# A filter dealt anew over the partitions of a spectral-mixing and feed-forward kernel, with a pause in SyncE's queue and three plane copies on VectorE

## The chip, the cores and the metric

The kernel runs on one core of one Trainium2 chip. The core has five engines with queues of their own: TensorE (matmuls, in the profile PE, its weight loads PEld), VectorE (DVE), ScalarE (ACT), GpSimd (POOL) and SyncE (SP), which here only issues DMAs. GpSimd issues DMAs as well. Sixteen DMA engines carry all transfers. Instructions of one queue run in order, and queues wait for each other by semaphores. The metric is the device time of one execution in microseconds, and the median of the runs is what is compared.

## The reference

The input x is 2048 rows of 576 bfloat16 values. The first part is a spectral mixing layer: layer norm over each row, a two-dimensional real Fourier transform over rows and columns, an elementwise product with a complex filter of 2048 x 289, the inverse transform, and a residual addition. The second part is a feed-forward block with a gate: layer norm, two products with 576 x 4608 weights, GELU of the one times the other, a product with 4608 x 576, and again a residual addition.

```
X = rfft2(layernorm(x));  X = X * (w_r + 1j * w_i)
h = x + irfft2(X)
n = layernorm(h)
out = h + (gelu(n @ w_gate) * (n @ w_up)) @ w_down
```

`w_r` and `w_i` are the two planes of the filter. They are inputs in device memory and have to be loaded.

## The kernel before, in words

Both transforms are written as matmuls with constant tables. The transform of length 2048 over the rows is split as 128 x 16: `A` stages (line 551) make 64 frequencies with 128-row tables while x is loaded and normalised; `D` (line 640) transforms over the columns, `B` (line 660) does the length-16 part with table BT, `T` (line 673, VectorE) multiplies by the filter, `V` and `R` (lines 681 and 698) go back over the length-16 part with table VT, `I` (line 835) goes back over the columns, and `N` (line 852) over the rest of the rows. After that come the second layer norm, the gate and up products (line 944) and the down product (line 1044).

Work between `B` and `V` is done in 16 groups; group number g runs from 1 to 15 and then 0. The filter lies in the tile WS as [partition, jp, plane, g, column]. The 128 partitions are two halves of 64, and jp (0 or 1) says which half's rows a DMA brings. Of the 64 rows of a half, 32 are "up" rows, which lie in memory in rising order of g and are brought by `w_up` (line 449), and 32 are "down" rows, in falling order, brought by `w_down` (line 456), 16 rows in a DMA, one for each of four slots `sl`. Row g = 0 of the down rows has its own DMAs, `w_zero` (line 464). Before, the up rows lie on the first 32 partitions of a half and the down rows on the other 32. Where a row lies must agree with the tables BT and VT, whose rows are put in the same order in `build_tables` (line 143).

The filter comes in two halves of g (`hf`): g 0 to 8 first (call it the first filter half), g 9 to 15 second. `T` needs the whole filter on all 128 partitions for both jp, so every half of 64 partitions is copied to the other one by `dup_w` (line 719), in four pieces k of g: k = 0 is g 1 to 5, k = 1 is g 6 to 8, k = 2 is g 9 to 12, k = 3 is g 13 to 15 and 0. Piece 0 is copied by engines (line 728 VectorE, line 730 GpSimd), one instruction per jp and plane; pieces 1 to 3 are copied by DMAs that GpSimd issues (line 242 is the helper by which every DMA is issued).

The order of the work is written out by hand in strings of tokens (`SEQ1`, `SEQF`, `SEQ`). Each engine gets its instructions in program order, and `Prog.emit` puts a wait before an instruction for each last writer or reader of what it touches. All DMAs under one semaphore name count on one semaphore, so a reader waits for all of that name issued so far.

SyncE's queue around the change is: loads of x and the table ATB, the tables FT and BT, the first filter half (plane 1, then plane 0), part of VT, the second filter half, the zero rows; then three small transfers VR<-RB of the transform's remaining columns; then, in `tab_load` (line 754), a wait for the last `dup_w` DMA and the tables VT, DT, IT and IDT; then six more VR<-RB, and the feed-forward weights. GpSimd's queue is: copies and scaling for the first layer norm, two loads of the second filter half (plane 0, slots 2 and 3), the two copies of piece 0 for plane 1, the two DMAs of piece 1, seven small operations (line 745), the six DMAs of pieces 2 and 3, and then its share of VR<-RB. VectorE copies piece 0 of plane 0 (two instructions) after the last U casts (line 562) and before the casts and products of the `D` to `V` stages.

Of the kernel before, what the change touches and what calls it, by code (L numbers as in the profile page):

```python
# [9 lines left out]
S, D, K2 = 2048, 576, 289  # L10
# [36 lines left out]
def build_tables():  # L47
# [52 lines left out]
    for st in range(2):  # L100
        g = 1 - st
        for p in range(128):
            half, r, jj = p // 64, (p % 64) // 4, p % 4
            low = (g + 16 * jj) if half == 0 else _minus_rows(g)[jj]
            k = 128 * r + low
            w = np.exp(-2j * np.pi * ((k * nn) % 2048) / 2048.0)
            if low in (0, 64):
                sl, ri = 0, (0 if low == 0 else 1)
# [8 lines left out]
            if half == 0:  # L117
                sl = jj
                e = np.exp(-2j * np.pi * ((r * nn) % 16) / 16.0)
                ca, cb = e, 1j * e  # L120
            else:
                sl = (128 - low - g) // 16
# [17 lines left out]
    for st in range(2):  # L140
        for jp in range(2):
            for q in range(64):
                half, r, sl = q // 32, (q % 32) // 2, 2 * jp + q % 2
                jj = sl if half == 0 else (4 - sl) % 4 if st else 3 - sl
                po, cut = 64 * half + 4 * r + jj, slice(2 * jp, 2 * jp + 2)
                for m in range(2):
                    for ri in range(2):
                        BN[jp, :, :, st, m, ri, q] = B[st, m + ri, :, cut, :, po].reshape(16, 4)
                for ri in range(2):
                    VN[st, jp, ri, q, 0] = V[st, ri, po, :, :, cut].reshape(2, 16, 4)  # L150
                    VN[st, jp, ri, q, 1] = (1 - 2 * ri) * V[st, 1 - ri, po, :, :, cut].reshape(2, 16, 4)
# [180 lines left out]
def _build(nc, A_x, A_w_r, A_w_i, B_w_gate, B_w_up, B_w_down, out):  # L332
    P = Prog(nc)
    T = build_tables()
    dram = {n: nc.inline_tensor(_np_bf16(T[n]), name="c_" + n.lower()) for n in T}
    PE, DVE, ACT, SP, POOL = "pe", "dve", "act", "sp", "pool"
# [12 lines left out]
    WS = sb.alloc("WS", [128, 2, 2, NG, K2], BF16)  # L349
# [96 lines left out]
    P.dma(SP, FT[:, :, :].rearrange("p a b -> p (a b)"), dram["FTAB"][:, :], "ft", w=["FT"])  # L446
    P.dma(SP, BT[:, :, :, :].rearrange("p a b c -> p (a b c)"), dram["BTAB"][:, :], "bt", w=["BT", "BT1"])

    def w_up(pl, hf):
        g0, g1 = ((0, 9), (9, 16))[hf]  # L450
        src = (A_w_r, A_w_i)[pl].tensor
        for jp in range(2):
            P.dma(SP, WS[64 * jp:64 * jp + 32, jp, pl, g0:g1, :].rearrange("p g k -> p (g k)"),
                  bass.AP(src, (32 * jp + g0) * K2, [[128 * K2, 16], [16 * K2, 2], [1, (g1 - g0) * K2]]), f"w{pl}{hf}", w=[("W", hf, pl, jp)])

    def w_down(pl, hf, sls=(0, 1, 2, 3), eng=SP, sem=""):
        g0, g1 = ((1, 9), (9, 16))[hf]
        src = (A_w_r, A_w_i)[pl].tensor
        for sl in sls:
            p0 = 64 * (sl // 2) + 32  # L460
            P.dma(eng, WS[p0 + sl % 2:p0 + 32:2, sl // 2, pl, g0:g1, :], bass.AP(src, (64 + 16 * (3 - sl) + 16 - g0) * K2, [[128 * K2, 16], [-K2, g1 - g0], [1, K2]]),
                  f"w{pl}{hf}{sem}", w=[("W", hf, pl, 2 + sl)])

    def w_zero(pl):
        for jp in range(2):
            P.dma(SP, WS[64 * jp + 32:64 * jp + 64, jp, pl, 0, :], bass.AP((A_w_r, A_w_i)[pl].tensor, (64 + 32 * jp) * K2, [[128 * K2, 16], [(-16 if jp else 48) * K2, 2], [1, K2]]),
                  f"wz{pl}", w=[("W", 2, pl, jp)])

    for pl in (1, 0):
        w_up(pl, 0)  # L470
        w_down(pl, 0)
    P.dma(SP, VT[:, 0:2, :, :].rearrange("p a b c -> p (a b c)"), dram["VTAB"][:, 0:512], "vt", w=["VT", "VT1"])
    for pl in (1, 0):
        w_up(pl, 1)
        w_down(pl, 1, (0, 1, 2, 3) if pl else (0, 1))
    for pl in (1, 0):
        w_zero(pl)
    GORD = list(range(1, NG)) + [0]
    wkeys = [[("W", hf, pl, h) for pl in range(2) for h in range(6 if hf < 2 else 2)] for hf in range(3)]

# [109 lines left out]
    for t, w in enumerate(SEQF):  # L592
        k, i = w[0], w[1:].rstrip("abc")
# [125 lines left out]
    def dup_w(k, jp, pl=slice(0, 2), eng=None):  # L719
        a, b = 64 * jp, 64 - 64 * jp  # L720
        n = ("Wd", k, jp, pl.start)
        for g0, g1 in (((1, 6),), ((6, 9),), ((9, 13),), ((13, 16), (0, 1)))[k]:
            dst, src = (WS[q:q + 64, jp, pl, g0:g1, :].rearrange("p a g k -> p a (g k)")[:, :, 1:] for q in (b, a))
            r = [x for x in (wkeys[1] if g0 > 8 else wkeys[0] if g0 else wkeys[0] + wkeys[2]) if pl.start <= x[2] < pl.stop]
            if eng is None:
                op = P.dma(POOL, dst, src, f"wd{k}{jp}", r=r, w=[(*n, g0)])
            elif eng == DVE:
                P.op(DVE, lambda v: v.tensor_copy(dst, src), r=r, w=[(*n, g0)])
            else:
                P.op(POOL, lambda v: v.tensor_scalar(dst, src, 1.0, 1.0, op0=ALU.mult, op1=ALU.mult), r=r + [("ATS", NT - 1)], w=[(*n, g0)])  # L730
        return op if eng is None else None

    w_down(0, 1, (2, 3), POOL, "p")
    for jp in range(2):
        dup_w(0, jp, slice(1, 2), POOL)
        dup_w(0, jp, slice(0, 1), DVE)
    for jp in range(2):
        dup_w(1, jp)
    c = 0
    while c < NT:  # L740
        c1 = c + 1
        while c not in ACT_TILES and c1 < NT and c1 not in ACT_TILES:
            c1 += 1
        src, f, keys = (SA[:, 0, c:c1], -1.0 / D, "SA0") if c in ACT_TILES else (MV1[:, c:c1, 0], -1.0, "MV1")
        P.op(POOL, lambda g, c=c, c1=c1, src=src, f=f: g.tensor_scalar(NM[:, c:c1], src, f, 1.0, op0=ALU.mult, op1=ALU.mult),
             r=[(keys, k) for k in range(c, c1)], w=[("NM", k) for k in range(c, c1)])
# [63 lines left out]
    for t, w in enumerate(SEQ):  # L810
        k, i = w[0], int(w[1:].rstrip("ADSP"))
# [207 lines left out]
    for j, c in enumerate(range(NPRE, NT)):  # L1019
        f = DEF0 + DSTEP * j  # L1020
# [77 lines left out]
def bass_sequential_preLN__spectral_gfnet__geglu_ffn__prompt_kernel(  # L1098
    nc, A_x, A_w_r, A_w_i, B_x, B_w_gate, B_w_up, B_w_down, out
):  # L1100
    _build(nc, A_x, A_w_r, A_w_i, B_w_gate, B_w_up, B_w_down, out)
# [28 lines left out]
```

## Time and profile before

| | |
|---|---|
| median of 3 runs | 485.8 us (484.93 to 485.94) |
| profiled execution | 486.04 us, span 484.2 us |
| granted TensorE clock | 1.00 |
| PE busy | 477.1 us (99%) |
| VectorE, ScalarE, GpSimd busy | 182.8, 145.4, 53.2 us |
| DMA | 33.19 MB in 28438 packets |

The span runs from the first to the last instruction of the program; the profiled execution's own time has 1.8 us around it. Lines L123 are those of the kernel's source. In a timeline row stand the start, the duration, the engine, the line, the operation, what is written and read, the shapes and the count, and in square brackets how long the engine had been idle and what ended that. SPq is SyncE's queue. In the chain of waits stand the start, the duration and what the time went to. In the groups of DMA issues stand the count, the size of each, and the median time from issue to landing.

### The profile page before, as it was taken

To read this page: it belongs to the slowest core of one execution; us is meant where nothing else is said; L and a number is where in the kernel's file an instruction comes from. 1 tells how busy PE (TensorE), PEld (TensorE's weight loads), DVE (VectorE), ACT (ScalarE), POOL (GpSimd) and SP (SyncE) were. 2 spreads that over 40 slices of the span, in tenths; PEclk is the share of its full clock that TensorE was granted. 3 is DMA by queue.
4 is the path that set the end of the run, shared out by engine and by line. 5 is a ranking of instruction groups with operands and counts; after the bars stand their busy time and mean duration, and the time that the engine had idled before them with its cause. 6 is when DMAs were issued, how large, how long until landed. Compare 5 with 4: busy or idle time off the path is not lost.

```text
span 484.2 us, 12888 instructions
## 1 busy us (share of the span) xinstructions
PE 477.1 (99%) x5874; PEld 279.1 (58%) x5874; DVE 182.8 (38%) x365; ACT 145.4 (30%) x291; POOL 53.2 (11%) x88
## 2 busy tenths in 40 slices
PE   7999999999999999999999999999999999999998
PEld 4877765544577644444677544444777444444774
DVE  7988755665500144333200234333101233333011
ACT  6998753434300032233200133223100133223000
POOL 7862317010120000000000000000000000000000
PEclk9999999999999999999999999999999999999999
DMA  8955789931430001000000011000000000000000
GB/s 289 217 134 161 249 283 346 333 87 24 161 111 27 26 15 23 20 1 0 3 14 15 26 24 22 14 0 2 3 14 26 14 1 0 1 1 1 3 26 26
DMA packets 28438, 33.19 MB, mean 69 GB/s; under 512 B 12624, under 2 KB 21472, under 8 KB 28384
## 3 DMA queue, kind: packets, MB, share of 16 engines
q1 hardware_dynamic: 24720, 19.87, 14.5%
q0 software_dynamic: 3664, 12.50, 8.0%
q8 instruction: 46, 0.75, 0.7%
q14 instruction: 8, 0.07, 0.1%
HBM read 26.21 MB, written 2.36 MB: 59 GB/s over the span
## 4 chain that ended last, share of the span: by engine, by line
PE 91%; SPq 3%; DMA 2%; DVE 2%; ACT 1%; issue 0%; DVEq 0%
PE PS L944 58%; PE PS L1044 27%; SPq L242 3%; PE PS L1056 2%; DMA WS<-in_A_w_r_dram 1%; PE PS L640 1%; DMA VR<-RB 1%; PE PS L994 1%; DVE XO L858 1%; PE PS L681 1%; ACT YS L606 1%; PE PS L835 0%; PE PS L660 0%; PE PS L1011 0%; PE PS L852 0%
## 5 line engine op out<-in xcount | busy, mean ns | idle before, releaser
L944 PE MATMUL PS<-HT,WG 64*128 64x512 bf16 (+1 forms) x2142 | 233.3, 372 | 0.1
L944 PEld LDWEIGHTS PS<-HT,WG 64*128 64x128 bf16 x2142 | 105.8, 94 | 114.5 <-DVE AT L953 0.2
L952 ACT ACTIVATE GL<-PS 128x512 bf16<-128x512 f32 x144 | 85.7, 596 | 281.7 <-PE PS L944 281.7
L953 DVE TENSOR_TENSOR AT<-GL,PS 128x512 bf16<-128x512 bf16 x144 | 98.8, 687 | 166.0 <-ACT GL L952 166.0
L1044 PE MATMUL PS<-WD,AT 64*128 64x288 bf16 x2160 | 132.9, 283 | 0.0
L1044 PEld LDWEIGHTS PS<-WD,AT 64*128 64x128 bf16 x2160 | 102.5, 94 | 30.6
L1031 DVE TENSOR_TENSOR OS<-PS,XO 128x288 bf16<-128x288 f32 (+2 forms) x32 | 13.3, 453 | 125.5 <-PE PS L1044 118.0
L944 PE MATMUL PS<-HT,WGX 64*128 64x512 bf16 x486 | 53.4, 376 | 0.0
L944 PEld LDWEIGHTS PS<-HT,WGX 64*128 64x128 bf16 x486 | 23.0, 94 | 29.4
L861 ACT ACTIVATE OS<-XO,NM 128x576 bf16<-128x576 bf16 x15 | 11.6, 774 | 11.4 <-DVE XO L1015 11.4
L640 PE MATMUL PS<-FT,U 64*128 64x288 bf16 x160 | 13.7, 284 | 0.3 <-DVE V L606 0.2
L673 DVE TENSOR_TENSOR TP<-YS,WS 128x1024 bf16<-128x1024 bf16 x16 | 11.0, 688 | 1.0 <-PE PS L698 1.0
L494 DVE BATCH_NORM_STATS2 ST<-XO 128x6 f32<-128x288 bf16 x26 | 10.1, 442 | 1.9 <-DMA XO<-in_A_x_dram 1.8
L681 PE MATMUL PS<-VT,TP 64*128 64x128 bf16 x256 | 10.0, 217 | 0.0
L242 POOL DMA_DIRECT2D WG<-in_B_w_gate_dram x9 | 6.1, 679 | 32.2 <-DMA WG<-in_B_w_gate_dram 28.9
L562 ACT ACTIVATE U<-PS 128x384 bf16<-128x384 f32 (+2 forms) x27 | 9.4, 479 | 0.7 <-PE PS L551 0.7
L242 POOL DMA_DIRECT2D WD<-in_B_w_down_dram x9 | 6.7, 755 | 26.1 <-PE PS L1011 26.1
L551 PE MATMUL PS<-ATS,XO 128*128 128x128 bf16 x96 | 8.3, 219 | 1.4 <-POOL ATS L520 1.4
L606 ACT ACTIVATE CUS<-PS 128x576 bf16<-128x576 f32 x14 | 9.0, 654 | 0.7 <-PE PS L640 0.5
L606 ACT ACTIVATE YS<-PS 128x576 bf16<-128x576 f32 x14 | 8.9, 653 | 0.6 <-PE PS L660 0.4
L1056 PE MATMUL PS<-WD,AT 128*128 128x448 bf16 (+1 forms) x72 | 9.0, 286 | 0.0
L681 PEld LDWEIGHTS PS<-VT,TP 64*128 64x128 bf16 x256 | 8.0, 94 | 1.3
(89 smaller groups left out, 230.0 us busy)
## 6 DMA issues: line engine op xcount, KB each, us to landing
WD<-in_B_w_down_dram POOLq DMA_DIRECT2D x9, 576.0 KB, 10.7
WG<-in_B_w_up_dram SPq DMA_DIRECT2D x6, 576.0 KB, 6.4
WG<-in_B_w_gate_dram POOLq DMA_DIRECT2D x6, 576.0 KB, 5.7
out_dram<-OS SPq DMA_DIRECT2D x30, 72.0 KB, 1.7
XO<-in_A_x_dram SPq DMA_DIRECT2D x6, 288.0 KB, 4.5
WGX<-in_B_w_up_dram SPq DMA_DIRECT2D x2, 576.0 KB, 4.7
WGX<-in_B_w_gate_dram POOLq DMA_DIRECT2D x2, 576.0 KB, 5.8
HT<-HN SPq DMA_TRANSPOSE x60, 2.4
```

The costliest lines, as they stand in the source:

```text
L242: fn = lambda e: e.dma_start(out_ap, in_ap)
L606: fn = (lambda v: v.tensor_copy(dst, src)) if eng == DVE else (lambda a: a.activation(dst, src, ACTF.Copy))
L640: return P.op(PE, lambda t: t.matmul(bank(b0 + o, 0, 128, 0, 2 * HK), U[64 * h:64 * h + 64, us, 2 * i:2 * i + 2, :, :], FT[64 * h:64 * h + ...
L673: P.op(DVE, lambda v, dst=dst, y4=y4, w4=w4: v.tensor_tensor(dst, y4, w4, op=ALU.mult), r=[("Y", sl), *dup[(i >= 5) + (i >= 8) + (i >= 12) ...
L681: return P.op(PE, lambda t: t.matmul(bank(b0 + o, 0, 128, 128 * c, 128 * c + 128), TP[64 * h:64 * h + 64, z, o, t_, c:256:2], VT[64 * h:64 ...
L861: P.op(ACT, lambda a, c=c, out=out: a.activation(out, XO[:, c, 0:D], ACTF.Square, bias=NM[:, c:c + 1], accum_out=SB2[:, 1, c:c + 1]), r=[( ...
L944: op = P.op(PE, lambda t, h0=h0, kt=kt, wt=wt, b=b, s=(not second and j == 0), e=(second and j == n - 1): t.matmul(bank(b, 0, 128, c0, c1) ...
L952: P.op(ACT, lambda a: a.activation(GL[:, s2, :], bank(b0), ACTF.Gelu_apprx_tanh), r=[("PS", b0)], w=[("GL", s2)])
L953: P.op(DVE, lambda v: v.tensor_tensor(AT[:, f, :], GL[:, s2, :], bank(b0 + 1), op=ALU.mult), r=[("GL", s2), ("PS", b0 + 1)], w=[("AT", f)])
L1031: P.op(DVE, lambda v: v.tensor_tensor(OS[:, p % 2, d0:d1], bank(b, 0, 128, 0, d1 - d0), XO[:, c, d0:d1], op=ALU.add), r=[("PS", b), ("X", ...
L1044: e[h] = P.op(PE, lambda t, f=f, h=h, r0=r0, j=j: t.matmul(bank(b0 + h, 0, 128, 0, 288), AT[r0:r0 + 64, f, 128 * p:128 * p + 128], WD[r0:r ...
L1056: P.op(PE, lambda t, b=b, d0=d0, d1=d1, f=f, j=j: t.matmul(bank(b, 0, 128, 0, d1 - d0), AT[:, f, 128 * p:128 * p + 128], WD[:, f, d0:d1], ...
```

## The change

The diff has five parts. Rows of the filter are dealt anew: of the 64 partitions of a half, the even ones hold up rows and the odd ones hold down rows, and the down rows of the two slots of a half alternate. The tables follow. DMAs of the two partition halves take turns in SyncE's queue (`w_up` now issues one DMA; slots go 0, 2, 1, 3). After the first DMA of the second filter half, SyncE waits until the whole first filter half is there. VectorE copies three of the four planes of piece 0 instead of two, GpSimd one instead of two. GpSimd issues its two loads of the second filter half after the DMAs of piece 1 instead of before its copies.

```diff
@@ build_tables
-                half, r, sl = q // 32, (q % 32) // 2, 2 * jp + q % 2
+                half, r, sl = q % 2, q // 4, 2 * jp + q // 2 % 2
@@ _build
-    def w_up(pl, hf):
+    def w_up(pl, hf, jp):
         g0, g1 = ((0, 9), (9, 16))[hf]
         src = (A_w_r, A_w_i)[pl].tensor
-        for jp in range(2):
-            P.dma(SP, WS[64 * jp:64 * jp + 32, jp, pl, g0:g1, :].rearrange("p g k -> p (g k)"),
-                  bass.AP(src, (32 * jp + g0) * K2, [[128 * K2, 16], [16 * K2, 2], [1, (g1 - g0) * K2]]), f"w{pl}{hf}", w=[("W", hf, pl, jp)])
-
-    def w_down(pl, hf, sls=(0, 1, 2, 3), eng=SP, sem=""):
+        P.dma(SP, WS[64 * jp:64 * jp + 64:2, jp, pl, g0:g1, :].rearrange("p g k -> p (g k)"),
+              bass.AP(src, (32 * jp + g0) * K2, [[128 * K2, 16], [16 * K2, 2], [1, (g1 - g0) * K2]]), f"w{pl}{hf}", w=[("W", hf, pl, jp)])
+
+    def w_down(pl, hf, sl, eng=SP, sem=""):
         g0, g1 = ((1, 9), (9, 16))[hf]
         src = (A_w_r, A_w_i)[pl].tensor
-        for sl in sls:
-            p0 = 64 * (sl // 2) + 32
-            P.dma(eng, WS[p0 + sl % 2:p0 + 32:2, sl // 2, pl, g0:g1, :], bass.AP(src, (64 + 16 * (3 - sl) + 16 - g0) * K2, [[128 * K2, 16], [-K2, g1 - g0], [1, K2]]),
-                  f"w{pl}{hf}{sem}", w=[("W", hf, pl, 2 + sl)])
+        jp, p0 = sl // 2, 64 * (sl // 2) + 2 * (sl % 2) + 1
+        P.dma(eng, WS[p0:64 * jp + 64:4, jp, pl, g0:g1, :], bass.AP(src, (64 + 16 * (3 - sl) + 16 - g0) * K2, [[128 * K2, 16], [-K2, g1 - g0], [1, K2]]),
+              f"w{pl}{hf}{sem}", w=[("W", hf, pl, 2 + sl)])
...
     for pl in (1, 0):
-        w_up(pl, 0)
-        w_down(pl, 0)
+        for jp in range(2):
+            w_up(pl, 0, jp)
+        for sl in (0, 2, 1, 3):
+            w_down(pl, 0, sl)
     P.dma(SP, VT[:, 0:2, :, :].rearrange("p a b c -> p (a b c)"), dram["VTAB"][:, 0:512], "vt", w=["VT", "VT1"])
-    for pl in (1, 0):
-        w_up(pl, 1)
-        w_down(pl, 1, (0, 1, 2, 3) if pl else (0, 1))
+    w_up(1, 1, 0)
+    P.op(SP, None, after=[o for k in wkeys[0] for o in P.last_w[k]])
+    w_up(1, 1, 1)
+    for sl in (0, 2, 1, 3):
+        w_down(1, 1, sl)
+    for jp in range(2):
+        w_up(0, 1, jp)
+    for sl in (0, 2):
+        w_down(0, 1, sl)
     for pl in (1, 0):
         w_zero(pl)
...
-    w_down(0, 1, (2, 3), POOL, "p")
-    for jp in range(2):
-        dup_w(0, jp, slice(1, 2), POOL)
-        dup_w(0, jp, slice(0, 1), DVE)
+    dup_w(0, 0, slice(1, 2), POOL)
+    for jp, pl in ((1, 1), (0, 0), (1, 0)):
+        dup_w(0, jp, slice(pl, pl + 1), DVE)
     for jp in range(2):
         dup_w(1, jp)
+    for sl in (1, 3):
+        w_down(0, 1, sl, POOL, "p")
```

`w_zero` writes every second partition of a half likewise.

More of the change, by code (lines that the diff above doesn't have):

```diff
@@ L464, in w_zero @@
     def w_zero(pl):
         for jp in range(2):
-            P.dma(SP, WS[64 * jp + 32:64 * jp + 64, jp, pl, 0, :], bass.AP((A_w_r, A_w_i)[pl].tensor, (64 + 32 * jp) * K2, [[128 * K2, 16], [(-16 if jp else 48) * K2, 2], [1, K2]]),
+            P.dma(SP, WS[64 * jp + 1:64 * jp + 64:2, jp, pl, 0, :], bass.AP((A_w_r, A_w_i)[pl].tensor, (64 + 32 * jp) * K2, [[128 * K2, 16], [(-16 if jp else 48) * K2, 2], [1, K2]]),
                   f"wz{pl}", w=[("W", 2, pl, jp)])
+    wkeys = [[("W", hf, pl, h) for pl in range(2) for h in range(6 if hf < 2 else 2)] for hf in range(3)]
@@ L478, in _build @@
     GORD = list(range(1, NG)) + [0]
-    wkeys = [[("W", hf, pl, h) for pl in range(2) for h in range(6 if hf < 2 else 2)] for hf in range(3)]
     def act_sum(c):
```

## The prediction

> **What bounds the kernel now.** I read the page first, then the chain that ended last, then the first 45 us engine by engine, because everything the change touches lies there.
>
> ```profile
> span 484.2 us, 12888 instructions
> ...
> PE 91%; SPq 3%; DMA 2%; DVE 2%; ACT 1%; issue 0%; DVEq 0%
> ```
>
> From about 45 us on the kernel is TensorE work back to back, and the change does not alter one matmul. So its worth is the shift of the moment when that dense part starts. The chain of waits up to there:
>
> ```profile
> 13.77 6.59 DMA WS<-in_A_w_r_dram
> 20.38 0.53 DVE WS L728
> ...
> 21.50 0.63 DVE CUS L606
> ...
> 27.36 0.12 PE PS L698 x4
> 27.51 0.70 DVE TP L673
> ...
> 40.12 0.23 SPq L242
> ...
> 41.02 3.68 DMA VR<-RB
> 44.70 0.46 issue
> 45.16 1.08 PE PS L835 x14
> ```
>
> Four things are on it: the last DMA of the first filter half (issued 13.77, there at 20.36), the two VectorE copies behind it, a VectorE product at 27.51, and at the end SyncE's queue with a small VR transfer that lands at 44.70. The last is the surprising one: the row-transform stage at 45.16 waits for SyncE, not for arithmetic.
>
> ```profile
> 6.00:12.00 6.00, 4.63 (x53) 3.11 (x52) 5.98 (x26) 4.66 (x17) 4.68 (x10) 1.00 0.96 361
> 12.00:16.00 4.00, 4.00 (x72) 3.86 (x70) 3.92 (x16) 4.00 (x15) 3.44 (x5) 1.00 1.10 239
> 16.00:20.40 4.40, 4.40 (x78) 3.94 (x76) 3.31 (x14) 4.18 (x13) 4.13 (x5) 1.00 1.08 204
> 28.00:36.00 8.00, 7.80 (x170) 6.02 (x166) 7.63 (x21) 7.19 (x16) 7.00 (x14) 1.00 0.65 161
> 36.00:44.00 8.00, 7.55 (x202) 6.30 (x198) 7.81 (x21) 7.66 (x19) 3.84 (x8) 1.00 0.56 167
> ```
>
> In these stages (time, then busy PE, PEld, DVE, ACT, POOL, granted clock, DMA share, GB/s) the DMA engines are full from 6 to 20.4 us, but move 361 GB/s while whole-height tiles load and only 239 and 204 while filter rows load. After 28 us PE, VectorE and ScalarE are each over 89% busy: a balanced stage, in which no single engine's gain passes through whole.
>
> **The change, part by part.** The rows for VectorE, TensorE, GpSimd and SyncE, in this order:
>
> ```profile
> 16.93 2.40 DVE L562 CAST U<-PS 128x384 bf16<-128x384 f32 x6
> 20.38 1.07 DVE L728 COPY WS<-WS 64x1444 bf16<-64x1444 bf16 x2 [1.05 <-DMA WS<-in_A_w_r_dram]
> 27.51 0.70 DVE L673 TENSOR_TENSOR TP<-YS,WS 128x1024 bf16<-128x1024 bf16 x1 [0.95 <-PE PS L698]
> 34.38 0.68 DVE L673 TENSOR_TENSOR TP<-YS,WS 128x1024 bf16<-128x1024 bf16 x1
> 37.67 0.69 DVE L673 TENSOR_TENSOR TP<-YS,WS 128x1024 bf16<-128x1024 bf16 x1
> 18.86 2.04 PE L640 MATMUL PS<-FT,U 64*128 64x288 bf16 x30
> 16.03 1.34 POOL L242 DMA_DIRECT2D WS<-in_A_w_r_dram  x2
> 17.44 2.86 POOL L730 TENSOR_SCALAR WS<-WS 64x1444 bf16<-64x1444 bf16 x2
> 20.64 1.54 POOL L242 DMA_DIRECT2D WS<-WS  x2 [0.34 <-DMA WS<-in_A_w_r_dram]
> 27.89 3.59 POOL L242 DMA_DIRECT2D WS<-WS  x6 [2.55 <-DMA WS<-in_A_w_r_dram]
> 15.04 4.92 SPq L242 DMA_DIRECT2D WS<-in_A_w_i_dram  x6
> 20.00 2.92 SPq L242 DMA_DIRECT2D WS<-in_A_w_r_dram  x4
> 24.51 1.38 SPq L242 DMA_DIRECT2D WS<-in_A_w_r_dram  x2
> 29.04 2.00 SPq L242 DMA_DIRECT2D VR<-RB  x3
> 36.12 0.33 SPq L242 DMA_DIRECT2D VT<-c_vtab  x1
> 37.94 4.30 SPq L242 DMA_DIRECT2D VR<-RB  x6
> ```
>
> ```profile
> WS<-in_A_w_i_dram SPq DMA_DIRECT2D x2, 162.6 KB, 7.2
> WS<-in_A_w_i_dram SPq DMA_DIRECT2D x4, 72.2 KB, 6.9
> ```
>
> *Dealing and alternation.* Same bytes, same number of DMAs; the tables BT and VT only change their contents. The question is when the first half is complete. Its 1.26 MB (two planes, each of the DMAs in these two rows) take 5.7 us at 220 GB/s, between the two measured rates. If halves in turn gave the 361 GB/s of the loads before, it would be 3.5 us, 2.2 us earlier. If dealing does nothing, it stays at 20.36. GpSimd's two loads of 63.2 KB at 16.03, now later, no longer share the engines: 0.13 MB at 204 GB/s is 0.6 us, of which some 0.4 falls before 20.36; I count it inside the range rather than on top. Ends 18.0 and 20.4; a small loss cannot be excluded, but no row shows one. I take the middle, 19.2, since both rates are rows of the same engines equally full.
>
> The Trainium skill, "SBUF — State Buffer", Door 1, says that a DMA on partitions 0 to 63 reaches the same eight of sixteen ports as one on 0 to 31. The drop from 361 to 204–239 GB/s at full engines agrees with eight ports. By that rule the new deal alone gains nothing, 20.4 stands, and the outcome is the slower rival below.
>
> *VectorE's third copy.* VectorE ends its U casts at 19.33 and sits until 20.38. Copies cost 0.53 each. The first (other plane) needs data that GpSimd already used at 17.44, so 19.33 to 19.86; the two others to 20.92. The cast of CUS behind them also needs the 30 matmuls that end at 20.90. So it starts at about 20.95 instead of 21.50 by the chain: 0.5 us gained. Cover gone (first half still at 20.36), the third copy still lies in the idle 1.05, and the gain is 0.
>
> *GpSimd.* One copy (1.43) goes, the two loads move behind the WS<-WS copies of the next rows. GpSimd is free at about 18.9, then waits for the first half: those copies are issued at about 19.3 instead of 20.64. They took 5.7 us to land:
>
> ```profile
> WS<-WS POOLq DMA_DIRECT2D x2, 216.5 KB, 5.7
> WS<-in_A_w_r_dram SPq DMA_DIRECT2D x2, 126.4 KB, 3.7
> WS<-in_A_w_r_dram SPq DMA_DIRECT2D x1, 63.2 KB, 5.7
> WS<-in_A_w_r_dram SPq DMA_DIRECT2D x2, 18.1 KB, 3.0
> SPq L242 <- DMA WS<-WS: 5.1, 1, 5.1
> L242 SPq DMA_DIRECT2D WS<-in_A_w_i_dram x14: 577/612/1732, 6.4 to 23.9; - x14
> ```
>
> The second went out at about 21.6 (the pair ends at 22.18, a copy's issue takes 0.6) and so landed at about 27.4, just before the product at 27.51. The row names PE as the releaser of its 0.95 us, but that matmul does not feed the product; the copy does. Issued by 20.1 and landing 5.7 later, 25.8, it is in time, and the 0.95 goes. Together with the 0.5 VectorE is up to 1.4 us ahead; in the balanced stage I let 1.0 pass.
>
> *SyncE's pause.* This is the price. Before, the second half was queued from 15.04;  the last load that the next GpSimd copies need, the fourth of those from 20.00 to 22.92, went at about 21.9 and landed 5.7 later at 27.6. Now all but one wait until 19.2. Behind the wait stand 9 second-half loads, 4 zero-row loads, then three VR transfers, the tables and six more VR. Nine loads at 0.65 (0.612 and a gap): the ninth goes out at 19.2 + 8 x 0.65 = 24.4. Landing between 3.0 (the small ones) and 5.7 (the full queue): the queue is emptier, so 3.4, between the 3.0 and 3.7 rows: 27.8, 0.2 later than before. The last zero rows go out at 27.0 and land at 30.0; GpSimd needs them for its fourth of the six copies, at 28.1 + 3 x 0.6 = 29.9: covered within 0.1. SyncE is free at 27.7, ahead of the VR transfer that went at 29.04.
>
> GpSimd's six WS<-WS copies thus start at 28.1 instead of 27.89. The first two served the product at 34.38, the rest the one at 37.67, and SyncE waits for the last (5.1 us, until 36.12) before tables and VR. From 36.12 SyncE issues without a pause until 42.24, and 44.70 follows. So the dense part shifts with that landing: +0.2, and VectorE's 1.0 us ends in waits at those products and at the VR transfer.
>
> *Sum.* The profiled execution took 486.04 us (span 484.2, 1.8 around it), 0.2 above the median 485.8. 486.04 + 0.2 = 486.2, on the median's scale 486.0.
>
> **The rivals.**
>
> *The gain passes (faster).* If alternation brings the rate near 361 GB/s, the half is there at 18.0; the ninth load goes at 23.2 and lands at 26.6; GpSimd's six copies start 1.0 earlier, SyncE's tables too, VectorE has its 1.0 to 1.4. All arms move together: −1.1, 484.7. For it: engines full at a lower rate. Against it: the first two loads of each plane already alternate before, and the average is 204 to 239 all the same. It needs the ninth load landed by about 26.7.
>
> *The pause decides (slower).* If dealing changes nothing, the half is there at 20.3, the ninth load goes at 25.5 and lands at 28.9 with 3.4, at 31.2 with 5.7. The six copies start 1.3 us late or more, the product that stood at 34.38 and SyncE's tables follow: +1.3, 487.1. It decides as soon as that landing passes 28.6. For it: every microsecond of pause goes straight down SyncE's full queue from 36.12 to 44.70. Against it: the issue of 15.04 to 25.89 contains stalls (up to 1.73 for one) that a pause may absorb.
>
> *The change doesn't do what it says*: the half complete at 20.3 but the landing of the loads behind it much shorter (3.0): +0.9, inside the range.
>
> **How the numbers follow.** The cancelling case 0.36, faster 0.32, slower 0.32. The first spreads from 485.1 to 486.8 (first half 0.7 us earlier or later), nearly all within 0.2% (1.0 us, about what a measurement of this kernel can tell from no change); I give 0.02 of it to each side. Of each rival 0.01 stays within. So faster 0.33, same 0.34, slower 0.33. For 8 in 10 the range takes in both rivals' points and leaves their far ends out: 484.4 to 487.3.
>
> **What would show it.** Right: VectorE's three copies back to back from 19.3 to 21; no idle time before the product that stood at 27.51; GpSimd's six copies near 28.1; SyncE's wait for WS<-WS ending near 36.3, and the stage of 45.16 near 45.4. Wrong on the fast side: those six copies before 27. Wrong on the slow side: the copies after 29.2, with VectorE idle before the product that needs them. If the dense part starts early although SyncE's tables do not, my claim that SyncE's queue holds it is false. What would upset all of it is a filter half that arrives later than 20.4.

## The result, and the profile after

The changed kernel is slower: 488.23 us median (485.80 to 488.71, 5 runs) against 485.80 us (484.93 to 486.05, 5 runs) before, a ratio of 1.0047 with an interval of 1.0032 to 1.0063. That lies above the predicted range of 484.4 to 487.3 and 2.2 us from the point, 486.0.

The profiled execution took 487.02 us, with a span of 485.2 us against 484.2. The chain of waits of the kernel after, up to the row transform (start, duration, what the time went to):

```profile
span 485.2 us, 12888 instructions
...
14.04 4.30 DMA WS<-in_A_w_r_dram
24.22 1.41 SPq L242
26.95 3.27 DMA WS<-in_A_w_r_dram
30.50 1.15 POOL WS L242 x2
31.66 5.25 DMA WS<-WS
...
42.15 3.56 DMA VR<-RB
46.17 1.08 PE PS L843 x14
```

The first row answers to the one of 13.77 before: the first filter half is there at 18.34 instead of 20.36. After that the chain is a new one. It goes through the last zero rows (out at 26.95, there at 30.22), the GpSimd copies of pieces 2 and 3 that wait for them, and the last of those copies (there at 37.24). Two arms leave that copy. The chain follows the one through VectorE's product at 37.33 and ScalarE's casts, but that product is not late: before, it stood at 37.67. The other arm is SyncE's: it issues the tables from 37.26 and the VR transfers behind them, with no break over 0.1 us until the last of them goes out at 42.15. That one lands at 45.71 instead of 44.70, and the row transform starts at 46.17 instead of 45.16.

The timeline of the kernel after, with the rows of VectorE, GpSimd, SyncE and TensorE that answer to those shown of before:

```profile
19.44 1.62 DVE L735 COPY WS<-WS 64x1444 bf16<-64x1444 bf16 x3
21.03 0.76 DVE L613 CAST CUS<-PS 128x576 bf16<-128x576 f32 x1
26.50 0.70 DVE L680 TENSOR_TENSOR TP<-YS,WS 128x1024 bf16<-128x1024 bf16 x1
37.33 0.69 DVE L680 TENSOR_TENSOR TP<-YS,WS 128x1024 bf16<-128x1024 bf16 x1 [0.42 <-issue]
27.94 1.85 POOL L242 DMA_DIRECT2D WS<-WS  x3 [4.37 <-DMA WS<-in_A_w_r_dram]
30.50 1.75 POOL L242 DMA_DIRECT2D WS<-WS  x3 [0.71 <-DMA WS<-in_A_w_r_dram]
37.26 0.33 SPq L242 DMA_DIRECT2D VT<-c_vtab  x1
39.06 4.03 SPq L242 DMA_DIRECT2D VR<-RB  x6
42.89 1.16 PE L843 MATMUL PS<-DT,V 64*128 64x288 bf16 x16 [0.34 <-DVE V L613]
46.17 0.35 PE L843 MATMUL PS<-DT,VR 64*128 64x288 bf16 x2 [2.12 <-DMA VR<-RB]
```

VectorE gains most of what was forecast: three copies back to back, the cast of CUS at 21.03 instead of 21.37 (in the timeline before; the chain of waits puts that cast at 21.50), the product that waited 0.95 at 27.51 now at 26.50 without a wait. TensorE's work ahead of the row transform starts 0.47 earlier (42.89 instead of 43.36). But the six GpSimd copies are now split in two, 0.71 apart, SyncE's tables go out 1.14 later (37.26, before 36.12), and TensorE's idle time before the row transform grows from 0.65 to 2.12 us: 1.01 because the transfer is later, 0.47 because TensorE comes earlier.

In the stages of the kernel after (stage, length, then busy PE, PEld, DVE, ACT, POOL with counts, granted clock, DMA share, GB/s):

```profile
12.00:16.00 4.00, 4.00 (x71) 3.86 (x72) 4.00 (x17) 4.00 (x14) 3.42 (x5) 1.00 1.10 268
16.00:20.40 4.40, 4.40 (x77) 3.96 (x76) 4.29 (x15) 4.18 (x14) 3.31 (x5) 1.00 0.52 134
44.00:47.00 3.00, 0.88 (x16) 0.85 (x14) 0.48 (x2) 0.45 (x2) 0.00 (x0) 1.00 0.67 179
```

The pause shows in the second row: the DMA engines, full at 1.08 before, are half idle at 0.52. That work is done later.

One thing this trace doesn't show. The profiled span is only 1.0 us longer, but the medians lie 2.4 apart. Three of the five runs, 488.23, 488.58 and 488.71 us, had a mean granted clock of 0.996; the two at 1.000 took 487.02 and 485.80, the second as fast as the kernel before. Where the lost clock lies is the subject of the second group of experiments.

### The profile page after: what moved, and what is told of

The parts are those of the page before. It is cut to its first block, busy times and chain, and to the rows that moved or that the text cites. A ratio compares the mean times of both kernels' runs of the same rounds, so it can differ in the third digit from the quotient of the medians.

```text
span 485.2 us, 12888 instructions
## 1 busy us (share of the span) xinstructions
PE 476.5 (98%) x5873; PEld 280.2 (58%) x5874; DVE 183.6 (38%) x366; ACT 145.4 (30%) x291; POOL 50.7 (10%) x87
## 4 chain that ended last, share of the span: by engine, by line
PE 89%; SPq 4%; DMA 3%; DVE 1%; issue 1%; ACT 1%; POOL 0%; DVEq 0%
PE PS L952 58%; PE PS L1052 27%; SPq L242 4%; PE PS L1064 2%; DMA WS<-in_A_w_r_dram 2%; DMA WS<-WS 1%; DMA VR<-RB 1%; PE PS L1002 1%; DVE XO L866 1%; PE PS L843 0%; PE PS L1019 0%; PE PS L860 0%; ACT V L613 0%; DVE OS L926 0%; PE PS L912 0%
```

## The experiments

Theory after the result: the pause alone makes the kernel slower, through SyncE's queue, and a longer TensorE gap then makes the clock drop in many runs. The rivals: the new deal and the turns slow a stage by themselves; or the third VectorE copy and GpSimd's new order do; or the lost clock has nothing to do with the gap.

### The pause taken away, and alone

Changed kernel without the pause:

```diff
-    P.op(SP, None, after=[o for k in wkeys[0] for o in P.last_w[k]])
```

> The changed kernel without SyncE's pause; all else stays. Theory 1 (the pause delays zero rows, so GpSimd's last copies, so SyncE's tables and VR transfers): GpSimd's last copies no longer wait (0.7 us in the changed kernel), SyncE's wait for them ends at 36.0 to 36.5 instead of 37.26, TensorE's gap before the row transform shrinks from 2.1 us to under 1.2, the span comes to 484.0 to 484.4, and all timed runs show clock 1.00, so the median is 485.7 to 486.2. Rival (the new deal or the third copy costs the time): the span stays at 485.2 and the median near 488. Rival (without the pause the loads of the second half slow GpSimd's first pair of DMA copies again): VectorE waits 0.5 us or more at its fifth product and the span is 484.4 to 485.2.

Measured: 485.71 us, 1.0011 (0.9998 to 1.0023). The profiled row transform starts at 45.30, after a gap of 1.57 (under 1.2 was expected), SyncE's tables go out at 36.50. All but one of 11 runs had a clock of 1.000; the one at 0.996 took 488.29. So the rest of the change costs nothing that shows, and the pause is what makes it slower.

The kernel before with the pause alone, at the same place in the queue:

```diff
...
+    w_up(1, 1, (0,))
+    P.op(SP, None, after=[o for k in wkeys[0] for o in P.last_w[k]])
+    w_up(1, 1, (1,))
     for pl in (1, 0):
-        w_up(pl, 1)
+        if pl == 0:
+            w_up(pl, 1)
```

> The kernel before with SyncE's pause alone, at the same place; deal, order of the DMAs, copies and GpSimd's order as before. Theory 1 (the pause costs): the first filter half comes at about 20.0, SyncE resumes there, the last zero rows land near 31.5, GpSimd's last copy near 38 and the last VR transfer near 46.5: the profiled span is 1.5 to 2.5 above the kernel before. VectorE has nothing of the lead that it has in the changed kernel, so TensorE's gap before the row transform is 1.5 to 2.5 us; where it passes 2 us the granted clock falls: median 487.5 to 489. Rival (only together with the new deal and copies is it slow): within 0.5 us of 485.3.

Measured: 488.60 us, 1.0071 (1.0044 to 1.0097). Here the first half came at 20.72, so everything moved further than in the changed kernel. In the chain of waits of this kernel:

```profile
13.78 6.94 DMA WS<-in_A_w_r_dram
23.28 1.55 SPq L242
26.80 2.85 DMA WS<-in_A_w_r_dram
30.59 4.57 DMA WS<-WS
...
43.22 3.75 DMA VR<-RB
47.43 1.90 PE PS L840 x14
```

The pause alone makes the same chain and all of the loss. It also answers the slower rival of the prediction (half there at 20.3, +1.3): with the half at 20.7, the row transform starts 2.3 later.

Zero rows ahead of the pause, in the changed kernel: the loop over `w_zero` is moved up, behind the VT load.

```diff
     P.dma(SP, VT[:, 0:2, :, :]...
+    for pl in (1, 0):
+        w_zero(pl)
     w_up(1, 1, 0)
     P.op(SP, None, after=...)
...
-    for pl in (1, 0):
-        w_zero(pl)
```

> The changed kernel with the four zero-row loads issued ahead of the pause, right after the table VT, where SyncE would sit idle. Theory 1: GpSimd's fourth copy does not wait for zero rows any more (minus 0.7 us), the last copy lands at 36.4 to 36.7 instead of 37.24, the span falls by 0.6 to 0.8 to 484.5, clock 1.00 in most runs, median 485.9 to 486.6. Rival (the ninth load of the second half is what counts, not the zero rows): no change, 485.2 and 488. Rival (the early zero rows push the first filter half back): the pause ends after 18.9 instead of 18.36, and half of the gain is lost.

The trace came out as expected, the time didn't. GpSimd's second wait is gone; its waits in this kernel, against two in the kernel after (engine, what it waited for, total, times, longest):

```profile
POOL WS L242 <- DMA WS<-in_A_w_r_dram: 4.8, 1, 4.8
```

SyncE's tables go out at 36.36, the row transform starts at 45.25 and the span is 484.3. So in the profiled execution the wait for the zero rows is what the pause costs. But that execution, 486.08 us, is the fastest of the twelve. The median is 488.74, 1.007 (1.0049 to 1.0092): 8 of 12 runs had a clock of 0.996 or 0.993, although the profiled gap was only 1.68, and even the four at 1.000 took 486.08 to 487.90. So sending the zero rows early doesn't take the loss away, and that they alone carry it holds for one trace only. No trace of a slower run was taken.

### The clock

SyncE's tables one stage later, in the changed kernel:

```diff
-LOADS = {"r0": "t", ...
+LOADS = {"r1": "t", ...
```

> The changed kernel with SyncE's wait for the last copy and the four tables behind the second group of VR transfers instead of ahead of it (token t from r0 to r1). Theory 1: those three VR transfers leave at about 33.8, the tables still at 37.3, the last three VR transfers at 39.1 instead of 40.9 and the last lands at about 43.5; the row transform then waits for the VR casts of VectorE and ScalarE (44.0) instead of 46.17: the span falls by 1.6 to 2.0 to about 483.4, below the kernel before, with clock 1.00 throughout, median 484.9 to 485.3. Rival (the row transform waits for something else, the tables or a cast): the span stays within 0.3 us of 485.2.

A miss: 488.99 us, 1.0067 (1.0045 to 1.0090), in place of a gain. Only three of SyncE's six VR transfers went ahead of the tables, which went out at 37.91. The last of SyncE's went out at 40.91, the last of GpSimd's at 41.60, while the big IT table (landed at 43.96) was under way, and they landed only at 46.71 and 46.87, 5.8 and 5.3 us later. The others sent between 39.7 and 41.1 took 3.7 to 4.1, so the table by itself doesn't explain it. The first filter half, too, came later here, at 19.47. But this profile caught what the others missed. The stages and the timeline of this kernel around its gap:

```profile
46.80:47.00 0.20, 0.00 (x0) 0.00 (x0) 0.00 (x0) 0.00 (x0) 0.00 (x0) 0.97 0.96 287
47.00:50.40 3.40, 3.19 (x28) 2.26 (x30) 0.92 (x2) 1.47 (x3) 0.00 (x0) 0.50 0.27 75
50.40:52.00 1.60, 1.54 (x26) 1.00 (x24) 1.42 (x3) 1.03 (x2) 0.00 (x0) 1.00 0.78 206
```

```profile
47.21 0.46 PE L843 MATMUL PS<-DT,VR 64*128 64x288 bf16 x2 [2.51 <-DMA VR<-RB]
47.45 0.71 PE L843 MATMUL PS<-DT,V 64*128 64x288 bf16 x4
...
50.74 0.42 PE L860 MATMUL PS<-GS,IT 64*128 64x288 bf16 x4
```

At the end of a gap of 2.51 us the granted clock goes to 0.50 for 3.4 us, and four matmuls take 0.71 instead of 0.42. The kernel before with the pause alone shows the same stretch in its stages, after a gap of 2.16:

```profile
46.80:47.20 0.40, 0.00 (x0) 0.00 (x0) 0.00 (x0) 0.00 (x0) 0.00 (x0) 1.00 1.00 186
47.30:50.60 3.30, 3.17 (x28) 2.35 (x30) 0.91 (x2) 1.47 (x3) 0.00 (x0) 0.50 0.32 83
50.80:52.00 1.20, 1.20 (x22) 0.81 (x18) 1.19 (x3) 0.80 (x2) 0.00 (x0) 1.00 0.86 187
```

What one such stretch costs can be read from the spans. From the start of the row transform to the end of the span it is 439.0 to 439.1 us in each of the twelve profiles with a clock of 1.000 (before 484.2 - 45.16, after 485.2 - 46.17). In the two profiles with the stretch it is 487.7 - 47.21 = 440.5 and 488.0 - 47.43 = 440.6: 1.5 us more. And 3.4 us at half clock, in a span of 486 us, make a mean clock of 0.9965, which is what the runs with 0.996 had.

The same subtraction gives an estimate of when the row transform started in runs without a trace: the span less 439.05, and 1.5 more for each 0.0035 of clock lost. By it the changed kernel started at 45.0 to 46.4 (median 46.2), the one without the pause at 44.0 to 46.0 (44.9), the one with early zero rows at 45.3 to 47.6 (46.6). So the pause costs about a microsecond in most runs, not in the profiled one alone. The starts of one kernel differ by 1.4 to 2.3 us, so the gap of a profile is not the gap of the other runs. And the kernel with early zero rows was profiled in the run that started earliest.

Now the gap broken up: the changed kernel with eight matmuls of 128 x 512 on zeros, four matmuls ahead of the gap in TensorE's queue, into a PSUM bank whose content nothing reads at that point. They are extra work; the output is the same.

```diff
+    def fill_mm(n):
+        b = next(b for b in (0, 2, 4, 6) if b not in [SLOT["I", c] for c in range(3)])
+        for _ in range(n):
+            P.op(PE, lambda t: t.matmul(bank(b), ZD[:, 0:128], ZD[:, :], start=True, stop=True), r=["ZD"], w=[("PS", b)])
...
+        if w == "I2":
+            fill_mm(8)
```

> The changed kernel with eight matmuls of 128x512 on zeros, whose output nobody reads, in TensorE's gap before the row transform waits for VR. Theory 2 (3 of 5 timed runs of the changed kernel showed a granted clock of 0.996 and 486.4 to 486.9 us of span against 484.0 and 485.2 at 1.00, because the idle gap of about 2 us lets the clock be granted lower for a while): all runs show 1.00 and a span of 485.0 to 485.6, so the median falls from 488.2 to about 487.1 although the profiled span does not. Rival (the lower clock comes from something else, chance or another stage): the share of runs at 0.996 stays, median 488.

Measured: 487.18 us, 1.0038 (1.0024 to 1.0051), and all six runs at a clock of 1.000. The stage of the gap in this kernel, where TensorE is busy 2.04 of 3 us in place of 0.88, and its timeline:

```profile
44.00:47.00 3.00, 2.04 (x13) 0.82 (x12) 0.18 (x1) 0.00 (x0) 0.00 (x0) 1.00 0.67 179
```

```profile
44.54 1.67 PE L975 MATMUL PS<-ZD 128*128 128x512 bf16 x7 [0.52 <-DVE VR L613]
46.14 0.42 PE L843 MATMUL PS<-DT,V 64*128 64x288 bf16 x4
47.77 0.35 PE L843 MATMUL PS<-DT,VR 64*128 64x288 bf16 x2 [1.21 <-DMA VR<-RB]
```

The idle time is now in two parts, 0.52 and 1.21 us, and the clock stays, even with the last VR transfer as late as 47.35 in this profile. None of six against three of five is little by itself. Together with the two traces, in which the clock falls at the end of this gap and nowhere else, it makes the gap the cause. The 1.9 us over the kernel before that remain are the later start of the row transform (the profiled execution itself took 488.65, the latest start of all profiles with 47.77).

Over all runs, the gap in the one profile of a kernel and the runs in which the clock was below 1.000: gaps up to 0.65, 0 of 159 runs (before, 92 runs; deal, turns and both; the three kernels with early tables); broken up (1.21 left), 0 of 6; 1.37 (copies alone), 2 of 10; 1.57 (no pause), 1 of 11; 1.68 (zero rows early), 8 of 12; 2.12 (the change), 3 of 5; 2.16 (pause alone), 3 of 7; 2.51 (tables late), 7 of 9.

The Trainium skill, "TensorE: Matmul & The Clock Gate", Part 1, says that the clock is half or full and is decided over windows of about 3.4 us; the trace agrees (0.50, for 3.4 us). Its section "Why this matters for your kernels" asks for no idle gaps above about 3 us; here gaps of 2.16 and 2.51 us were enough in the profiles, so the measurement is the stricter rule.

### The other parts, alone

The new deal on the kernel before, with the DMAs of the first half in the order of before and no pause. The diff's `build_tables`, `w_up`, `w_down` and `w_zero` are in it; against the changed kernel the order of the first half is undone:

```diff
         for jp in range(2):
             w_up(pl, 0, jp)
-        for sl in (0, 2, 1, 3):
+        for sl in range(4):
             w_down(pl, 0, sl)
```

> The kernel before with the new deal of the rows alone: the DMAs in the order of before, no pause, copies and GpSimd's order as before. By the rule of the ports (a DMA on 64 partitions with a stride reaches the same engines as one on 32) it changes nothing: first half complete at 20.2 to 20.9 us, as in the two profiles without the new deal (20.36 and 20.72), and the time within 0.1% of before. If the deal is what brought the half forward in the kernel with deal and turns together (18.79), the half is there at 18.3 to 19.5 and the time is 0 to 0.5 us lower.

The turns alone, with the rows dealt as before:

```diff
-        for sl in sls:
+        for sl in (sls if eng != SP else [x for x in (0, 2, 1, 3) if x in sls]):
```

> The kernel before with the down loads of the two partition halves in turn alone (slots 0, 2, 1, 3), rows dealt as before. If taking turns is what brought the half forward, it is complete at 18.3 to 19.5 us; if the deal did, at 20.2 to 20.9 us as before. Time 0 to 0.5 us lower in the one case, within 0.1% of before in the other. If both this kernel and the one with the deal alone stay above 20, it takes the two together.

Both together, the rest as before (the diff of the change without its pause and without the lines on copies and on GpSimd's loads):

> The kernel before with the new deal and the halves taking turns, without the pause, with the copies and GpSimd's order as before. Theory 1: the first filter half lands at 18.3 to 19.0 instead of 20.36, VectorE starts its copies at 19.3 to 19.5 and its cast at about 20.9; its fifth product still waits for GpSimd's copies; the tables and VR transfers stay within 0.3 us of before, so the time does too: 485.0 to 485.7, all clocks 1.00. Rival (the deal does nothing and GpSimd's later loads brought the half forward): the half lands at 20.0 or later. Rival (the new deal costs): over 486.

Measured, with the time from the issue of the last DMA of the first half to its landing:

| kernel | issued, landed | us | ratio |
|---|---|---|---|
| deal | 13.58, 18.86 | 485.35 | 0.9994 (0.9984 to 1.0004) |
| turns | 13.80, 18.57 | 485.16 | 0.9993 (0.9981 to 1.0006) |
| both | 13.88, 18.79 | 485.15 | 0.9990 (0.9981 to 0.9999) |

In the four kernels with neither (before, pause alone, and two below) that transfer took 6.10 to 6.94 us, 6.49 in the mean; here it took 5.28, 4.77 and 4.91. So either part alone brings the half forward by 1.2 to 1.7 us, and the two don't add. Each is one profile, and with the deal alone the turns are undone for the first half only: its second half still has them, so the deal's share isn't separated from theirs. With the pause on top (five kernels) it took 4.24 to 5.74, 4.85 in the mean, against 4.97 in the three with deal and turns but no pause: the pause doesn't make the half earlier.

The time hardly follows, and the timeline of the kernel with the deal alone shows one reason:

```profile
18.04 2.87 POOL L736 TENSOR_SCALAR WS<-WS 64x1444 bf16<-64x1444 bf16 x2
20.86 1.29 POOL L242 DMA_DIRECT2D WS<-WS  x2
19.83 2.03 DVE L734 COPY WS<-WS 64x1444 bf16<-64x1444 bf16 x2
```

VectorE starts its two copies at 19.83 without a wait, since the half is there, but they take 2.03 us instead of 1.07, and end at 21.86, later than before (21.45): the first ends only after GpSimd's copies of the same tile do, at 20.91. With turns alone the two take 1.93, with both parts 2.02. Where GpSimd makes only one copy, VectorE's three take 1.62 to 1.81. The Trainium skill, "SBUF — State Buffer", "Who interferes with whom", says that a VectorE copy and a GpSimd instruction can need the same port pair, which the first holds for its whole instruction; the trace agrees, with a first copy that ends 0.4 us after GpSimd's.

The copies and GpSimd's order alone, on the kernel before:

```diff
-    w_down(0, 1, (2, 3), POOL, "p")
-    for jp in range(2):
-        dup_w(0, jp, slice(1, 2), POOL)
-        dup_w(0, jp, slice(0, 1), DVE)
+    dup_w(0, 0, slice(1, 2), POOL)
+    for jp, pl in ((1, 1), (0, 0), (1, 0)):
+        dup_w(0, jp, slice(pl, pl + 1), DVE)
...
+    w_down(0, 1, (2, 3), POOL, "p")
```

> The kernel before with the last part alone: VectorE copies three planes, GpSimd one, and GpSimd's two loads go behind the copies of piece 1. The first half stays at about 20.4 us (or 20.0 with two loads fewer beside it), so VectorE's third copy lies in its idle time before it, and the product that stood at 27.51 no longer waits if the DMAs of piece 1 go out at 20.4 as before or earlier. GpSimd's own second-half loads go out 6 us later, at 22 to 23, and land by 27.5 to 28.5, at or just behind the 27.89 at which its six copies start. Time: 485.0 to 485.9, no difference that counts, since SyncE's queue still sets the start of the row transform.

Measured: 485.52 us, 1.0010 (0.9990 to 1.0030), as expected. VectorE's product comes at 26.45 instead of 27.51 and TensorE's work 0.97 earlier (42.39), but the last VR transfer only 0.2 earlier (44.47). All that VectorE wins turns into a gap, 1.37 us, and two of ten runs lost clock (487.69 and 489.86). That is the change's gain in small: work ahead of a fixed transfer gets faster, and pays with the clock.

### SyncE's tables earlier

If SyncE's queue holds the row transform, it should help to free SyncE sooner. Its wait ahead of the tables stands on the last of GpSimd's six copies; the tables need nothing of them. Bound to the second copy instead, on the kernel before:

```diff
-            last = dup_w(k, jp)
+            last = dup_w(k, jp) if k == 2 else (dup_w(k, jp), last)[1]
```

> The same move of the wait for the tables in the kernel before. Theory 1: the row transform then waits for VectorE's casts, which end at 44.43, instead of VR at 44.70: a gain of 0.2 to 0.4, median 484.9 to 485.2. The difference to the changed kernel without pause and with the same move (0.5 to 0.8 us) is what the new deal and the copies are worth. Rival: as for that kernel, VectorE waits for GpSimd's last copies, and the time is the same or longer than before.

Measured: 485.35 us, 0.9995 (0.9985 to 1.0004), just above the 484.9 to 485.2 expected, with a profiled span of 483.1. The same line on the changed kernel without its pause:

> The changed kernel without the pause, and with SyncE's wait ahead of the four tables put on the second of GpSimd's six copies instead of the last. Theory 1 (SyncE's queue of tables and VR transfers sets when the row transform starts, and VectorE's lead of 0.5 to 1 us stays there as a wait): the tables leave at about 33.3, the last VR transfers as soon as their cast is there (39.2), landing near 42.5 to 43; the row transform waits for the casts of VectorE and ScalarE at about 44: the span falls to 482.9 to 483.4, the median to 484.3 to 484.9, faster than both kernels, clocks 1.00. Rival (the tables, moved forward, slow GpSimd's last copies down, and VectorE waits for these): the span stays at 484 or more and VectorE shows an idle stretch of 0.5 us or more near 37.

Measured: 484.59 us, 0.9985 (0.9976 to 0.9994), all 12 runs at 1.000. This beats the kernel before by 0.15% and the changed kernel by more. In its timeline SyncE and TensorE read:

```profile
33.14 0.33 SPq L242 DMA_DIRECT2D VT<-c_vtab  x1
36.21 5.06 SPq L242 DMA_DIRECT2D VR<-RB  x6
42.34 1.16 PE L842 MATMUL PS<-DT,V 64*128 64x288 bf16 x16 [0.38 <-DVE V L612]
43.56 0.35 PE L842 MATMUL PS<-DT,VR 64*128 64x288 bf16 x2
```

The tables go out at 33.14, the VR transfers end before they are needed, and TensorE goes from one stage into the next without a gap. Only now does VectorE's gain pass: the two kernels with this line differ by 0.76 us in their medians and by 0.5 in their profiled spans (483.1, 482.6). That is what deal, turns, copies and GpSimd's order are worth together, though the intervals against the kernel before overlap.

The same line on the changed kernel with its pause:

> The changed kernel with its pause, but with SyncE's wait ahead of the tables bound to the second of GpSimd's six copies instead of the last. If the pause costs time only because it goes down SyncE's queue to the transfers that the row transform waits for, SyncE is free of the wait at 34.5 to 35.5 us instead of 37.24, the last small transfer lands at 43.2 to 44.4 instead of 45.71, TensorE's gap there is under 1.7 us instead of 2.12, the clock stays at 1.00 in nearly all runs, and the time is 484.4 to 485.4, under the kernel before. If the pause also costs by another way (VectorE's products behind the late copies), the time stays at 486 or more although the last transfer lands earlier.

Measured: 485.19 us, 0.9991 (0.9980 to 1.0002), all 12 runs at 1.000. In its timeline:

```profile
31.12 1.75 POOL L242 DMA_DIRECT2D WS<-WS  x3 [1.23 <-DMA WS<-in_A_w_r_dram]
33.31 0.33 SPq L242 DMA_DIRECT2D VT<-c_vtab  x1
44.60 0.34 PE L843 MATMUL PS<-DT,VR 64*128 64x288 bf16 x2 [0.37 <-DMA VR<-RB]
```

GpSimd waits even longer for the zero rows than in the kernel after, 1.23 us, and yet TensorE starts at 44.60 instead of 46.17 and the loss is gone. So the way of the pause into the time is SyncE's wait for the last copy. The pause may still cost something: without it TensorE started at 43.56, with the work ahead of that 0.73 earlier. In the ratios, 0.9991 against 0.9985, the difference is within the intervals.

## Why the prediction was wrong

**What bounds the kernel: right.** The dense part's start decides, and SyncE's queue sets that start. Start and span move together within 0.1 us in the twelve profiles at a clock of 1.000, and freeing SyncE earlier made the row transform start earlier with every other part left alone.

**Dealing and alternation: too cautious, but not where it failed.** I took 19.2 between 18.0 and 20.4; it was 18.34. The rule of the Trainium skill cited there ("SBUF — State Buffer", Door 1), by which the deal gains nothing and 20.4 stands, isn't borne out by the one profile of the deal without turns in the first half: there the half was complete at 18.86. The turns do as much. My reading of a higher rate for halves in turn was half right: 268 GB/s from 12 to 16 us instead of 239, not 361.

**VectorE's third copy and GpSimd: right.** The cast at 21.03 (20.95 foreseen), the fifth product without its wait. The 0.5 gained was counted from the chain's 21.50; in one and the same view it is 0.34. I let 1.0 us pass and had it end in waits at the VR transfer; so it did. I counted that as costing nothing.

**SyncE's pause: this step failed.** The sum has +0.2 for it. The ninth load landed at 27.65 (27.8 foreseen) and GpSimd's copies started at 27.94 (28.1 foreseen). The zero rows went out at 26.95 (27.0) and landed at 30.22 (30.0). So far it is nearly exact, in part by luck: the half came 0.86 earlier than assumed, but the ninth load took 4.1 us to land instead of 3.4, and the first zero-row DMA took 1.41 to issue instead of 0.65. But I called the zero rows "covered within 0.1", and they weren't: GpSimd was ready for its fourth copy at 29.79 and went on at 30.50. Its last copy went out 0.80 later than before and took 0.34 more to land, and SyncE's wait ended at 37.26 instead of the 36.3 I foresaw. So the term measured +1.0 in the profiled execution (by the estimate from spans, the median of the five runs starts 1.2 us after that of the kernel before), and that with an early half. The mechanism stood in the text as the slower rival, "goes straight down SyncE's full queue"; I tied it to a late first half and to the ninth load, when a full microsecond goes through with an early half, in the trace by way of the zero rows. Of my signs for being right, the copies, the product and the start of GpSimd's six copies all came true. They look at the head of that row of copies, and the loss is at its end.

**A term that was missing.** The sum has no price for TensorE's idle time itself. The gap of 0.65 became 2.12, and in three of five runs the mean clock fell by what one stretch of half clock for 3.4 us gives: 1.5 us more, by the spans of the two profiles that show such a stretch. 1.0 and 1.5 are about the 2.4 between the medians. VectorE's gain belongs to this term: it made the gap 0.47 longer.

**The rivals.** The faster one needed a half near 18.0 and the ninth load by 26.7; it got 18.34 and 27.65. All its arms were to move together, and SyncE's didn't. "Doesn't do what it says" is out: the half did come earlier, though not through the pause.

**What stays open.** Why the clock falls in one run and not in the next: the gap is known for one run of each kernel only. What holds the kernel back with the zero rows early, in the runs that started over a microsecond after the profiled one: they may have had a longer gap, too, which would fit how often they lost the clock, but no trace shows it. A clock of 0.993 would be two such stretches; the second was not seen in a trace.

## What to carry to other kernels

Before pausing a queue, list everything that is queued behind the pause and who waits for each item, down to the smallest transfer: here four loads of 18 KB were enough to hold up the last copies in the trace. An engine's idle time isn't free when the engine's clock depends on it; in this kernel, price a profiled gap on TensorE of 1.4 us or more with the chance of 1.5 us of lost clock, and don't speed up the work in front of a fixed wait. Bind a wait to what the waiting instruction needs: SyncE's tables stood behind copies they don't use, and only when that wait was moved did the other four parts of the change show as a gain (0.9985, against 0.9995 for the moved wait alone; with the wait in its old place 1.0011). And profile more than one run where runs of a kernel differ by more than the effect.

## What was not expected of the hardware

The granted clock fell to 0.50 for 3.4 us after TensorE gaps of 2.16 and 2.51 us, and the mean clock was below 1.000 in 2 of 10 runs of a kernel with a profiled gap of 1.37. Putting the DMAs of the two partition halves in turn, with the same bytes and the same number of DMAs, shortened the last landing from 6.1 to 6.9 us to 4.77; dealing the rows over every second partition, with turns in the second half alone, shortened it too (5.28). Each is one profile. Two transfers of 8 KB took 5.8 and 5.3 us to land (out at 40.91 and 41.60, there at 46.71 and 46.87), against 3.7 for the last one in the kernel before; what slowed them isn't shown. And a VectorE copy of 0.53 us took 1.47 when a GpSimd copy of the same tile was running.
